# Block-causal attention and a two-layer FFN on one core: pairs of heads in float32 on the two column halves, joined maxima and sums, and six blocks in the end phase

## The chip, the cores and the metric

The kernel runs on one core of a Trainium2 chip. TensorE (PE) multiplies matrices out of SBUF into PSUM (8 banks of 128 partitions x 512 float32), VectorE (DVE), ScalarE (ACT) and GpSimd (POOL) work element by element, and SyncE (SP) issues the DMAs. Each engine takes its instructions in the order in which the program wrote them and waits on semaphores for the others. The metric is the device time of one execution in microseconds (us); lower is better. All inputs and outputs are float32.

## The reference

Attention over 8 batches x 8 heads, 576 positions of 64, with a mask in blocks of 64; then an FFN with silu over the 4608 tokens.

```python
def attn(q, k, v):                            # (8, 8, 576, 64) float32
    scores = np.matmul(q, k.transpose(0, 1, 3, 2)) / 8
    block = np.arange(576) // 64
    scores = np.where(block[:, None] >= block[None, :], scores, -1e9)
    p = np.exp(scores - scores.max(-1, keepdims=True))
    return np.matmul(p / (p.sum(-1, keepdims=True) + 1e-9), v)

def reference(q, k, v, moe_w_in, moe_w_out):  # (512, 2048), (2048, 512)
    x = attn(q, k, v).transpose(0, 2, 1, 3).reshape(4608, 512)
    h = x @ moe_w_in
    return (h / (1 + np.exp(-h))) @ moe_w_out
```

## The kernel before

**Precision.** Almost every product is taken as three products of rounded parts: a float32 operand is split into a high part (a cast to fp32r on ACT) and a low part (the difference, on POOL), and PE adds high x high, high x low and low x high.

**Attention.** The first 128 queries of each head are done early by the classes First and Second. The other 448 queries of a head are a unit; there are 64 units (u0 to u63), two heads that are neighbours being a pair. Keys lie on the partitions, queries along the free axis, five segments of keys (SEG) of 448, 320, 192, 448 and 64 queries. A unit goes through these steps:
- load (L290): q and k from DRAM into qkraw, of which there is one buffer, in two halves; split_hi (L298, ACT), split_lo (L302 and L304, POOL): qh and ql.
- scores (L326, PE): into three PSUM banks S.
- max (L270, DVE): for each segment a reduction with transposition over 32 keys into Mx; max2: quad_fold (L279) joins the four quarters of the partitions in four reductions, four more (L341) write the result to each quarter, and a broadcast (L274) fills MR.
- sub (L351, L356, L358, DVE): T = S - MR; exp (L367, ACT): p; p_hi (L373, ACT) and p_lo (L381, L383, POOL): ph, pl; v_hi (L310) and v_lo (L313): vc, with the low part of v beside the high part in the columns.
- sums (L270 into Dx, DVE), and once per pair sums2 (L279 into Xd, L396, L398): the reciprocal rr.
- pv (L405, PE): nine matmuls into U, high parts in one half of its partitions, low in the other; lower (L410, ACT) and fold (L416, DVE) add the halves; mult (L274, L421, DVE) multiplies by rr.
- x_hi (L450), x_lo (L456): the FFN's operand x, in 16 tiles that are free again once their block is done. For blocks in LATER x goes to DRAM instead.

**FFN.** 18 blocks of 256 tokens. A step is 12 matmuls of the first layer (L652, into h) or of the second (L687, into o); between them stand silu (L659), g_hi (L665) and g_lo (L670). 14 blocks go step by step beside the attention, 448 steps in all. The other four (LATER) wait for the end phase.

**Order.** Up to unit 16 a table (ORDER) says what each engine's queue gets, word by word. From TABLE = 17 a loop writes one unit after the other and puts FFN steps among them: `pace` is what is left to reach an even share, three of them at the end of the unit, and `while len(x_free) < z.fresh(): ffn(1)` does more where no x tile is free. The steps that remain after the loop are written ahead of the end phase.

**End phase.** For the blocks put off, two layers with seven products in place of eight (Strassen's scheme in Winograd's form, on halves of the operands). First layer: an item (L1000) is seven products of six matmuls into PSUM tiles X, Y (both named S) and Z; ACT copies partial sums out (keep, L1005), DVE and POOL add (L849), ACT applies silu (L1013). Second layer: mult_c (L1111). The sums of operands that the scheme needs are made by prep_x, prep_s, prep_t and prep_g (L849 sums and low parts, L858 casts). Everything in this phase is written as `at(t, ...)` with a planned time t and then sorted by it; ITEM = 4.94 is the planned length of an item, and product 1 of an item opens the PSUM tile that the item before last used.

Of the kernel before, what the change touches and what calls it, by code (L numbers as in the profile page):

```python
# [20 lines left out]
P = 128  # L21
# [7 lines left out]
TB = 256  # L29
# [6 lines left out]
TABLE = 17  # L36
LAG = 2
LATER = (14, 15, 16, 17)
# [5 lines left out]
USE = (1, 2, 6, 5, 7, 3, 4)  # L44
# [81 lines left out]
u15.lower u18.load ffn u16.p_hi:0 u15.fold u16.p_hi:1 u16.p_lo:0 u16.v_hi u15.mult ffn u16.v_lo ffn silu u16.p_lo:1 u17.load_v  # L126
g_hi u16.p_hi:2 ffn g_lo u15.x_hi ffn u15.x_lo silu ffn u16.p_lo:2 g_hi g_lo
# [14 lines left out]
def attn_ffn(ctx: ExitStack, tc: tile.TileContext, qk, v, qk0, v0, qk1, v1, w_in, w_out, out):  # L142
# [138 lines left out]
    class Unit:  # L281
# [10 lines left out]
        def load_v(u):  # L292
            u.vraw = sp.tile([P, 512], F32, tag="vraw", name="vraw")[:, : 5 * D]
            nc.sync.dma_start(out=u.vraw, in_=v[u.b, u.h])
# [40 lines left out]

        def max2(u):
            X = sp.tile([32, NQB, 4], F32, tag="Xm", name="Xm")
            quad_fold(X, Mx, ALU.max)
            m = sp.tile([P, NQB], F32, tag="m", name="m")
            for a in range(4):  # L340
                nc.vector.tensor_reduce(out=m[32 * a : 32 * a + 32], in_=X, axis=AX.X, op=ALU.max)  # L341
            u.mb = MR[:, :NQ]
            bcast(u.mb, m, NQB)
# [41 lines left out]
        def sums(u):  # L385
            n = u.h % 2 * NQB
            for j, c, q0, w in SEG:
                ttr(Dx[:, n + q0 // 32 : n + q0 // 32 + w // 32, j], blocks32(u.p[:, c : c + w]), ALU.add)
# [11 lines left out]
        def pv(u):  # L400

            U = u.U = pU.tile([P, 512], F32, tag="U", name="U")[:, :NQ]
            for n, (i, pp, m) in enumerate(PV):
                j, c, q0, w = SEG[i]
                nc.tensor.matmul(U[:m, q0 : q0 + w], u.vc[:, j, :m], (u.ph, u.pl)[pp][:, c : c + w], start=n == 0, stop=n == 8)  # L405

# [286 lines left out]
    def output(blk, d, t):  # L693
        ot = sp.tile([P, DM], F32, tag="ot", name="ot", bufs=2)
        ((o, c),) = outs[blk][t]
        (nc.vector.tensor_copy if late else nc.scalar.copy)(ot, o)
# [38 lines left out]
    late = []  # L735
# [24 lines left out]
    units = [Unit(b, h) for b in range(B) for h in range(H)]  # L760
    for i in range(0, len(units), 2):
# [22 lines left out]
    total = 4 * len(steps)  # L784
    for i in range(TABLE, n + 2):
        u = units[i] if i < n else None
        w = units[i - 1] if i <= n else None
        z = units[i - 2] if i > TABLE else None
        pace = AHEAD + (total - TAIL - AHEAD) * (i + 1 - TABLE) // (n + 2 - TABLE) - count[0]
# [15 lines left out]
        if z and z.h % 2:  # L805
# [4 lines left out]
        if w:  # L810
            w.sums()
            w.pv()
        if u:
            u.v_hi()
            u.v_lo()
            if i + 1 < n:
                units[i + 1].load_v()
            u.sub()
        if w:
            w.lower()  # L820
        if u:
            for part in (u.exp, u.p_hi, u.p_lo):
                for k in range(3):
                    part(k)
        if w and w.h % 2:
            w.sums2()
        late.append(u)
        ffn(3)
        late.pop()
# [7 lines left out]
    for i in range(left):  # L837
        at(FULL * (i - left), ffn, 1)
# [7 lines left out]
    right = {}  # L846

# [9 lines left out]
    def parts(t, h, l, src, eng, lag=0.9):  # L857
# [3 lines left out]
    def ops(t, e, out, a, b, op):  # L861
        at(t, lambda: tt(e, out(), a(), b(), op))

# [23 lines left out]
    def prep_x(t, u):  # L887
# [8 lines left out]

        b11, b12, b21, b22 = q(0, 0), q(0, 1), q(1, 0), q(1, 1)

        def t2():
            if u:  # L900
                z["t"] = right["p"].tile([P, 2, TB], F32, tag="tx", name="tx")
            return z["t"] if u else b22()

        def hl(t, j, src, eng):
            p = pair(u, j)
            if u:
                t = max([t] + [u * span - ITEM + (USE.index(i) + 1) * ITEM / 7 + 0.02 for i in USE if ring[u - 1][i] == ring[u][j]])
            parts(t, p[:, :, 0], p[:, :, 1], src, eng)

        at(t, load, 0)  # L910
        at(t, load, 1)
        hl(t + 4.0, 1, b11, V)
        hl(t + 4.7, 2, b21, G)
        ops(t + 5.6, V, b11, b12, b11, SUB)
        hl(t + 5.4, 3, b22, V)
        ops(t + 6.3, V, b12, b22, b12, SUB)
        ops(t + 7.0, V, t2, b22, b11, SUB)
        two_ = (lambda: z["t"]) if u else b22
        ops(t + 7.7, V, b21, b21, two_, SUB)
        hl(t + 7.7, 6, two_, G)  # L920
        hl(t + 8.4, 5, b11, V)
        hl(t + 9.1, 7, b12, G)
        hl(t + 9.8, 4, b21, V)

    def prep_s(t, d):
# [3 lines left out]
        h21, l21 = [w[:, 0:2, cols(d, 1)] for w in wi]  # L929
        at(t, raw, z, 0)  # L930

        def q(i, j=None):
            return lambda: z[0].rearrange("p q (c m) -> p q c m", c=2)[:, i : i + 1 if j is None else j]

        def whole(f):
            tt((G, V)[f], z[0][:, 2 * f : 2 * f + 2].rearrange("p q (c m) -> p (q c) m", c=2), f32(wi[0][:, :, cols(d, f)]), f32(wi[1][:, :, cols(d, f)]), ADD)

        at(t, whole, 0)
        at(t, whole, 1)
        ops(t + 0.9, V, q(3), q(2), q(3), ADD)  # L940
        ops(t + 1.4, V, q(2), q(0), q(2), SUB)
        ops(t + 1.8, V, q(0), q(3), q(0), SUB)
        ops(t + 2.3, V, q(1), q(1), q(0), SUB)
        parts(t + 1.4, h21, l21, lambda: q(3)()[:, 0], V, 1.6)
        parts(t + 2.8, H, L, q(0, 3), G)

    def prep_t(t, d):
# [3 lines left out]
        B = [w[:, 2 * d : 2 * d + 2, :].rearrange("p f (n m) -> p (f n) m", n=2) for w in wo]  # L951
        at(t, raw, z, 0)

        def q(i, j=None):
            return lambda: z[0][:, i : i + 1 if j is None else j]

        at(t, lambda: tt(G, z[0], f32(B[0]), f32(B[1]), ADD))
        ops(t + 2.6, V, q(0), q(1), q(0), SUB)
        ops(t + 3.0, V, q(1), q(3), q(1), SUB)
        ops(t + 3.5, V, q(3), q(3), q(0), SUB)  # L960
        ops(t + 3.9, V, q(2), q(2), q(3), SUB)
        parts(t + 3.5, H[:, 0:2], L[:, 0:2], q(0, 2), V)
        parts(t + 4.4, H[:, 2:4], L[:, 2:4], q(2, 4), G)
# [11 lines left out]
    def item(t, u, d, k):  # L975
        z = {}
        e = d % HALFD
        stat = {
            1: [w[:, 0:2, cols(d, 0)] for w in wi],
            2: [w[:, 2:4, cols(d, 0)] for w in wi],  # L980
            4: [w[:, 2:4, cols(d, 1)] for w in wi],
            5: [w[:, 0:2, cols(d, 1)] for w in wi],
            6: [w[:, e, 0] for w in sv],
            3: [w[:, e, 1] for w in sv],
            7: [w[:, e, 2] for w in sv],
        }

        def prod(i, o):
            if i == 1:
                z["X"] = bank(k % 2)[:, :TB]  # L990
                z["g"] = [both(k) for k in range(2)]
            elif i == 2:
                z["Y"] = bank(2)[:, :TB]
            elif i == 5:
                z["Z"] = pU.tile([P, 512], F32, tag="U", name="Z")[:, :TB]
            x = pair(u, i)
            n = 0
            for c in range(2):
                for a, b in ((0, 0), (0, 1), (1, 0)):
                    nc.tensor.matmul(z[o], stat[i][a][:, c], x[:, c, b, :], start=i in (1, 2, 5) and n == 0, stop=n == 5, skip_group_check=True)  # L1000
                    n += 1

        def keep(e, name, o):
            z[name] = half("s1" if name == "s5" else name)
            (e.copy if e is A else e.tensor_copy)(z[name], z[o])  # L1005

        def add(e, q, a, b):
            tt(e, z["g"][q[0]][:, q[1]], z[a], z[b], ADD)

        def silu2(h):  # L1010
# [10 lines left out]
        p = ITEM / 7  # L1021
        for n, (i, o) in enumerate(((1, "X"), (2, "Y"), (6, "X"), (5, "Z"), (7, "X"), (3, "Z"), (4, "X"))):
            at(t + n * p, prod, i, o)
        at(t + p + 0.01, keep, A, "s1", "X")
        at(t + 2 * p + 0.01, add, V, (0, 0), "Y", "s1")
        at(t + 2.6 * p, silu2, 0)
        at(t + 3 * p + 0.01, keep, A, "s2", "X")
        at(t + 4 * p + 0.01, keep, V, "s5", "Z")
        at(t + 5 * p + 0.01, keep, A, "s3", "X")
        at(t + 5.6 * p, add, G, (1, 1), "s5", "s3")  # L1030
        at(t + 6 * p + 0.01, add, V, (1, 0), "Z", "s2")
        at(t + 6 * p + 0.45, silu2, 1)
        at(t + 7 * p + 0.1, save, 1)
        at(t + 7 * p + 0.15, silu21)
        at(t + 7 * p + 0.5, save, 0)

    at(-0.005, start_b)
    for u in range(nuse):
        if u == 0 or order[u] != order[u - 1]:
            prep_x(u * span - 14.0, u)  # L1040
        for e in range(HALFD):
            d = e + HALFD * (u >= NDBL)
            t = u * span + e * ITEM
            if u in (0, NDBL):
                prep_s(t - 6.5 - (u > 0) * 1.5, d)
            item(t, u, d, u * HALFD + e)
    for d in range(HALFD):
        prep_t(end_b - span - 13.0 + 6.0 * d, d)
        prep_t(end_b - span + 11.0 + 5.5 * d, HALFD + d)

    flat = lambda z: z.rearrange("p a b c -> p (a b c)")
    et = lambda z: z.rearrange("p (j e t) -> p j e t", e=2, t=P)
# [15 lines left out]
    def prep_g(t, blk, q, c, tag):  # L1068
# [135 lines left out]
```

## Time and profile before

| what | us |
|---|---|
| median of 2 runs | 1151.69 (1150.3 to 1153.09) |
| the profiled execution, its own time | 1154.32 |
| its span | 1152.6 |
| PE busy | 1057.3 |
| DVE busy | 948.2 |
| POOL busy | 829.2 |
| ACT busy | 793.9 |

The span is the time from the first instruction to the last in the profiled execution, and the execution's own time is 1.7 us longer. The mean granted clock of PE is 0.967 of full speed. Rows of groups read: line, engine, operation, output <- input by the program's names, shape, count, then busy time, mean ns of one, and the idle time before them with what ended it. L12 is line 12 of the kernel.

### The profile page before, as it was taken

Reading aid. Unit: us, or ns where it says so; the run is one execution under the profiler, and the core shown is the slowest. Engines: PE = TensorE matmul, PEld = TensorE weight load, DVE = VectorE, ACT = ScalarE, POOL = GpSimd, SP = SyncE. Lnnn points to the kernel's source line nnn. Section 1 sums busy time; section 2 is a strip of 40 time slices with the busy share of each in tenths; the row PEclk is TensorE's granted clock in tenths of the full one; section 3 lists DMA queues with packets and bytes.
Section 4 is the critical chain, followed back from the end, with each engine's and each line's share of the span. In section 5 each row is a group of like instructions: output and inputs, shape, how many; then the busy total and the mean of one; then the engine's idle time right before and its main releaser. Section 6 shows DMA issues by size and latency. Waiting matters only on the chain.

```text
span 1152.6 us, 21493 instructions
## 1 busy us (share of the span) xinstructions
PE 1057.3 (92%) x7348; PEld 966.5 (84%) x7348; DVE 948.2 (82%) x2513; ACT 793.9 (69%) x1294; POOL 829.2 (72%) x751
## 2 busy tenths in 40 slices
PE   9999999999989997999999779999999787677987
PEld 8888999999978886889989669889889687577887
DVE  7986799999699996999985789999992757879665
ACT  5776688889788877888884768888873454443332
POOL 5766699889969886798976678878773646655344
PEclk9999999999999998999999889999999899788999
DMA  7873333232232321313221222332312033132431
GB/s 272 274 251 107 80 82 82 59 82 59 63 91 49 90 57 41 90 49 92 67 73 45 55 71 66 84 88 58 99 46 64 22 124 107 48 121 66 119 92 56
DMA packets 61389, 102.06 MB, mean 89 GB/s; under 512 B 7264, under 2 KB 34400, under 8 KB 61280
## 3 DMA queue, kind: packets, MB, share of 16 engines
q1 hardware_dynamic: 61280, 100.69, 30.9%
q8 instruction: 58, 0.95, 0.3%
q14 instruction: 51, 0.42, 0.1%
HBM read 80.74 MB, written 19.92 MB: 87 GB/s over the span
## 4 chain that ended last, share of the span: by engine, by line
PE 45%; DVE 28%; issue 8%; ACT 7%; POOL 7%; DMA 4%; SPq 2%; POOLq 0%; DVEq 0%; ACTq 0%
PE h L652 15%; PE o L687 15%; PE U L405 5%; PE S L326 4%; DVE Mx L270 3%; DVE Dx L270 3%; DVE raw L849 3%; PE S L1000 2%; DVE rx L849 2%; DVE m L341 1%; DVE Xm L279 1%; DVE xu L416 1%; ACT p L367 1%; POOL pl L381 1%; DVE MR L274 1%
## 5 line engine op out<-in xcount | busy, mean ns | idle before, releaser
L652 PE MATMUL h<-x,wi 128*128 128x256 f32 x2688 | 349.5, 284 | 0.0
L652 PEld LDWEIGHTS h<-x,wi 128*128 128x128 f32 x2688 | 339.8, 191 | 8.5 <-issue 0.5
L687 PE MATMUL o<-wo,g 128*128 128x512 f32 x1296 | 328.9, 399 | 0.0
L381 POOL TENSOR_TENSOR pl<-p,ph 128x448 fp32r<-128x448 f32 (+1 forms) x192 | 225.7, 1202 | 86.6 <-ACT ph L373 86.5
L687 PEld LDWEIGHTS o<-wo,g 128*128 128x128 f32 x1296 | 238.5, 190 | 48.6 <-issue 0.7
L670 POOL TENSOR_TENSOR g<-g,g 128x512 fp32r<-128x512 f32 x112 | 145.4, 1298 | 57.9 <-ACT g L665 42.7
L270 DVE TRANSPOSE_TENSOR_REDUCE Mx<-S 64x4 f32<-64x128 f32 (+4 forms) x384 | 132.9, 401 | 57.2 <-PE S L326 57.0
L270 DVE TRANSPOSE_TENSOR_REDUCE Dx<-p 128x14 f32<-128x448 f32 (+3 forms) x320 | 122.5, 445 | 0.1
L367 ACT ACTIVATE p<-T 128x512 f32<-128x512 f32 (+1 forms) x192 | 106.9, 605 | 19.7 <-POOL ph L383 14.0
L405 PE MATMUL U<-ph,vc 128*128 128x448 f32 (+3 forms) x320 | 78.8, 312 | 34.4 <-DVE xu L421 22.3
L302 POOL TENSOR_TENSOR qh<-qkraw,qh 64x576 fp32r<-64x576 f32 x64 | 91.7, 1433 | 18.0 <-ACT qh L298 9.1
L373 ACT CAST ph<-p 128x512 fp32r<-128x512 f32 (+1 forms) x192 | 104.0, 596 | 0.7 <-PE U L405 0.5
L659 ACT ACTIVATE g<-h 128x512 f32<-128x512 f32 x112 | 67.0, 598 | 47.4 <-POOL g L670 31.6
L367 ACT ACT_TABLE_LOAD x60 | 77.0, 1283 | 28.1 <-DVE T L356 26.8
L405 PEld LDWEIGHTS U<-ph,vc 128*128 128x128 f32 x320 | 59.1, 196 | 44.0 <-POOL ph L383 27.9
L326 PE MATMUL S<-qh 128*128 128x448 f32 (+3 forms) x320 | 91.1, 297 | 1.0 <-DVE T L356 0.7
L665 ACT CAST g<-g 128x512 fp32r<-128x512 f32 x112 | 69.4, 620 | 22.2 <-PE o L687 20.2
L326 PE MATMUL S<-ql,qh 128*128 128x448 f32 (+3 forms) x320 | 83.8, 306 | 0.0
L659 ACT ACT_TABLE_LOAD x64 | 82.1, 1283 | 1.1
L298 ACT CAST qh<-qkraw 128x1024 fp32r<-128x1024 f32 x64 | 66.8, 1044 | 16.8 <-DMA qkraw<-in_qk_dram 13.4
L304 POOL TENSOR_TENSOR ql<-qkraw,qh 128x448 fp32r<-128x448 f32 x64 | 74.1, 1158 | 5.0
L358 DVE TENSOR_TENSOR T<-S,MR 128x256 f32<-128x256 f32 (+2 forms) x192 | 72.9, 405 | 0.0
(206 smaller groups left out, 1959.5 us busy)
## 6 DMA issues: line engine op xcount, KB each, us to landing
qkraw<-in_qk_dram SPq DMA_DIRECT2D x128, 256.0 KB, 3.9
vraw<-in_v_dram SPq DMA_DIRECT2D x64, 160.0 KB, 3.0
gd<-g SPq DMA_DIRECT2D x32, 256.0 KB, 2.1
wst<-in_moe_w_out_dram SPq DMA_DIRECT2D x15, 512.0 KB, 5.0
rx<-gd SPq DMA_DIRECT2D x44, 128.0 KB, 2.7
wst<-in_moe_w_in_dram SPq DMA_DIRECT2D x10, 512.0 KB, 5.2
out_dram<-ot SPq DMA_DIRECT2D x17, 256.0 KB, 2.9
v<-in_v_dram SPq DMA_DIRECT2D x12, 256.0 KB, 5.9
```

What stands on the lines that cost most here:

```text
L270: nc.vector.tensor_reduce(out=out, in_=in_, axis=AX.X, op=op, apply_transpose=True)
L302: nc.gpsimd.tensor_tensor(out=u.qh[64:, NQ:], in0=u.raw[64:, NQ:], in1=u.qh[64:, NQ:], op=ALU.subtract)
L304: nc.gpsimd.tensor_tensor(out=u.ql, in0=u.raw[:, :NQ], in1=u.qh[:, :NQ], op=ALU.subtract)
L326: nc.tensor.matmul(u.ps(c, w, m), u.kk[:, j * P : j * P + m], qq[:, q0 : q0 + w], start=i == 0, stop=i == 1)
L367: nc.scalar.activation(u.p[:, c:e], T[:, c:e], AF.Exp, scale=SCALE)
L373: nc.scalar.copy(u.ph[:, c:e], u.p[:, c:e])
L381: nc.gpsimd.tensor_tensor(out=u.pl[:, c:e], in0=u.p[:, c:e], in1=u.ph[:, c:e], op=ALU.subtract)
L405: nc.tensor.matmul(U[:m, q0 : q0 + w], u.vc[:, j, :m], (u.ph, u.pl)[pp][:, c : c + w], start=n == 0, stop=n == 8)
L652: nc.tensor.matmul(h[:, f, :], wi[wt][:, c, w], x[:, xt, :], start=n == 0, stop=n == 3 * CT - 1)
L659: nc.scalar.activation(g, hs.pop((blk, d)), AF.Silu)
L670: nc.gpsimd.tensor_tensor(out=g2[:, 1], in0=g, in1=g2[:, 0], op=ALU.subtract)
L687: nc.tensor.matmul(o, g2[:, gt, f, tk], wo[wt][:, 2 * d + f, c], start=d == 0 and n == 0, stop=d == NSTEP - 1 and n == 5,)
```

## The change

From unit 16 on (PAIRED) neither p nor v is split. p stays in float32, in three buffers in turn (those that p, ph and pl had), and pv2 multiplies both heads of a pair at once: each head's v (64 columns) takes one half of PE's columns. U then holds both heads, and neither lower nor fold is needed. Maxima: one reduction over Mx (max_x), three copies on POOL that bring the other three quarters of the partitions beside the first (gather), one reduction (max_m), three copies back. Sums: the same with sums_x, gather and sums_m, where POOL also adds. split_lo of the next unit comes after these instead of before the FFN steps. mult2 multiplies out of PSUM. `late` becomes `by_vector`, and `late` now counts the steps at the unit's end.

Six blocks are put off instead of four: 384 FFN steps remain in the loop, and the end phase has 24 items in each layer instead of 16. Its products come in the order 1, 6, 5, 2, 7, 3, 4, with product 1 of an item three slots earlier, among the last products of the item before. The sums of prep_x, prep_s, prep_t and prep_g are written into PSUM (quad, with hold and wait to plan who has which bank), low parts from there are made by DVE, and most additions move to DVE.

```diff
-LATER = (14, 15, 16, 17)
+PAIRED = 16
+LATER = (12, 13, 14, 15, 16, 17)
-USE = (1, 2, 6, 5, 7, 3, 4)
+USE = (1, 6, 5, 2, 7, 3, 4)
...
+        def gather(u, z):
+            for a in range(1, 4):
+                nc.gpsimd.tensor_copy(out=z[:32, a], in_=z[32 * a : 32 * a + 32, 0])
+
+        def max_x(u):
+            u.mj = MR[:, 448:504].rearrange("p (a b) -> p a b", a=4)
+            nc.vector.tensor_reduce(out=u.mj[:, 0], in_=Mx, axis=AX.X, op=ALU.max)
+
+        def max_m(u):
+            u.m = sp.tile([P, NQB], F32, tag="m", name="m")
+            nc.vector.tensor_reduce(out=u.m[:32], in_=u.mj[:32].rearrange("p a b -> p b a"), axis=AX.X, op=ALU.max)
+            for a in range(1, 4):
+                nc.gpsimd.tensor_copy(out=u.m[32 * a : 32 * a + 32], in_=u.m[:32])
...
+        def sums_x(u):
+            u.dj = ident[:, : 8 * NQB].rearrange("p (a b) -> p a b", a=4)
+            nc.vector.tensor_reduce(out=u.dj[:, 0], in_=Dx, axis=AX.X, op=ALU.add)
+
+        def sums_m(u):
+            z, rs = u.dj, sp.tile([P, NQB], F32, tag="rs", name="rs")
+            t = MR[:32, 960:1016].rearrange("p (a b) -> p a b", a=2)
+            u.rs = rs
+            nc.gpsimd.tensor_tensor(out=t, in0=z[:32, 0:2], in1=z[:32, 2:4], op=ALU.add)
+            nc.gpsimd.tensor_scalar(out=t[:, 0], in0=t[:, 0], scalar1=1e-9, scalar2=None, op0=ALU.add)
+            for a in range(4):
+                n = slice(NQB * (a // 2), NQB * (a // 2) + NQB)
+                nc.gpsimd.tensor_tensor(out=rs[32 * a : 32 * a + 32], in0=t[:, 0, n], in1=t[:, 1, n], op=ALU.add)
...
-                u.p = sp.tile([P, COLS], F32, tag="p", name="p")
+                u.p = sp.tile([P, COLS], F32, tag=("p", "ph", "pl")[max(0, u.i - PAIRED) % 3], name="p")
...
+        def pv2(u):
+
+            U = u.U = pU.tile([P, 512], F32, tag="U", name="U")[:, :NQ]
+            for n, (j, c, q0, w) in enumerate(SEG[i] for i in (0, 3, 1, 2, 4)):
+                for e, z in enumerate((u.mate, u)):
+                    nc.tensor.matmul(U[64 * e : 64 * e + 64, q0 : q0 + w], z.vv[:, j], z.p[:, c : c + w], start=n == 0, stop=n == 4)
+
+        def mult2(u):
+
+            bc = MR[:, 512 : 512 + NQ]
+            bcast(bc, u.rr, NQB)
+            u.xu = sp.tile([P, 512], F32, tag="xu", name="xu")[:, :NQ]
+            nc.vector.tensor_tensor(out=u.xu, in0=u.U, in1=bc, op=ALU.mult)
...
-        pace = AHEAD + (total - TAIL - AHEAD) * (i + 1 - TABLE) // (n + 2 - TABLE) - count[0]
+        pace = max(0, AHEAD + (total - TAIL - AHEAD) * (i + 1 - TABLE) // (n + 2 - TABLE) - count[0])
+        late = min(pace, 2 if i % 2 == 0 else 3)
         if u:
             u.scores()
             u.max()
-        if z:
-            z.fold()
-            if z.h % 2:
-                z.mult()
-        if u:
-            u.max2()
-        if i + 1 < n:
-            units[i + 1].split_hi()
-            units[i + 1].split_lo()
+            u.max_x()
+            u.gather(u.mj)
+        if nxt:
+            nxt.split_hi()
             if i + 2 < n:
                 units[i + 2].load()
-        ffn(pace - 3)
...
+        ffn(pace - late)
+        if w:
+            w.sums(2)
+        if u:
+            u.max_m()
+        if w:
+            w.sums(-3)
+        if done:
+            done.pv2()
+            done.sums_x()
+            done.gather(done.dj)
+            done.sums_m()
+        if nxt:
+            nxt.split_lo()
+        if u:
+            u.max_b()
+            u.sub()
+        if z:
+            z.sums_r()
+            z.mult2()
...
+    def quad(t, z, q, kind, where, outs):
...
+        t = wait(where, t)
+        hold(where, t + 3.15)
+        at(t, start)
+        if kind == "S":
+            ops(t + 0.5, V, x(0), x(3), q(3), ADD)
+            ops(t + 0.9, V, x(1), q(0), x(3), SUB)
+            ops(t + 1.3, V, x(2), x(0), q(0), SUB)
+            ops(t + 1.7, V, x(3), q(1), x(2), SUB)
...
+        for i, o in ((1, "X"), (6, "X"), (5, "Z"), (2, "Y"), (7, "X"), (3, "Z"), (4, "X")):
+            at(t + USED[i] * p7 - ITEM * (i == 1), prod, k, i, o)
```

Where instructions stand now, at three places. POOL's queue through one unit of the steady loop, before (pl and ph: the low parts of p; g: that of the FFN's g; qh and ql: those of the next unit's k and q; vc: that of v):

```order
L302 TENSOR_TENSOR qh<-qkraw,qh 64x576
L304 TENSOR_TENSOR ql<-qkraw,qh 128x448
L313 TENSOR_TENSOR vc<-vraw,vc 128x5x64
L381 TENSOR_TENSOR pl<-p,ph 128x448
L381 TENSOR_TENSOR pl<-p,ph 128x512
L381 TENSOR_TENSOR pl<-p,ph 128x448
L383 TENSOR_TENSOR ph<-p,ph 64x64
L670 TENSOR_TENSOR g_7766<-g,g_7766 128x512
L302 TENSOR_TENSOR qh<-qkraw,qh 64x576
```

and after, in an even unit (MR holds the maxima of the four quarters, m the joined ones, ident the sums, rs their total):

```order
L352 COPY MR<-MR 32x14 x3
L362 COPY m<-m 32x14 x3
L352 COPY ident<-ident 32x28 x3
L376 TENSOR_TENSOR MR<-ident 32x56
L377 TENSOR_SCALAR MR<-MR 32x28
L380 TENSOR_TENSOR rs<-MR 32x14 x4
L316 TENSOR_TENSOR qh<-qkraw,qh 64x576
L318 TENSOR_TENSOR ql<-qkraw,qh 128x448
```

The low parts of p and v are gone; qh and ql, which the next unit's scores read, now stand behind fifteen small operations on maxima and sums.

PE's queue from the end of unit 28's scores, before (S: scores, U: p times v, h: FFN):

```order
L326 MATMUL S_5894<-ql,qh 64x64
L405 MATMUL U<-ph,vc 128x448
L405 MATMUL U<-ph,vc 128x320
L405 MATMUL U<-ph,vc 128x192
L405 MATMUL U<-pl,vc 64x192
L405 MATMUL U<-pl,vc 64x320
L405 MATMUL U<-pl,vc 64x448
L405 MATMUL U<-ph,vc 128x64
L405 MATMUL U<-pl,vc 64x448
L405 MATMUL U<-ph,vc 128x448
L652 MATMUL h<-x,wi_78 128x256 x2
```

and after, from the end of unit 30's scores to the start of unit 31's:

```order
L340 MATMUL S_5806<-ql,qh 128x192
L340 MATMUL S_5807<-qh 64x64
L340 MATMUL S_5807<-ql,qh 64x64
L462 MATMUL U<-p,v 64x448 x4
L462 MATMUL U<-p,v 64x320 x2
L462 MATMUL U<-p,v 64x192 x2
L462 MATMUL U<-p,v 64x64 x2
L340 MATMUL S_5880<-qh 128x448
```

Before, FFN steps follow the product p·v; after, no step stands between the scores of unit 28 and those of unit 32 but the products of a pair, as 25 steps were written into unit 27.

PE's queue at the end of an item of the first layer, before (Z and S: the PSUM tiles; the second S number is the next item's):

```order
L1000 MATMUL Z<-x,sv_11387 128x256 x2
L1000 MATMUL Z<-x,sv_11388 128x256
L1000 MATMUL S_11589<-x,wi_78 128x256 x2
L1000 MATMUL S_11589<-x,wi_79 128x256
L1000 MATMUL S_11589<-x,wi_78 128x256 x2
L1000 MATMUL S_11589<-x,wi_79 128x256
L1000 MATMUL S_11660<-x,wi_78 128x256 x2
L1000 MATMUL S_11660<-x,wi_79 128x256
L1000 MATMUL S_11660<-x,wi_78 128x256 x2
```

and after:

```order
L1127 MATMUL S_10013<-x,wi_78 128x256 x2
L1127 MATMUL S_10013<-x,wi_79 128x256
L1127 MATMUL S_10013<-x,wi_78 128x256 x2
L1127 MATMUL S_10013<-x,wi_79 128x256
L1127 MATMUL Z<-x,sv_9748 128x256 x2
L1127 MATMUL Z<-x,sv_9749 128x256
L1127 MATMUL Z<-x,sv_9748 128x256 x2
L1127 MATMUL Z<-x,sv_9749 128x256
L1127 MATMUL S_9955<-xown,wi_78 128x256 x2
L1127 MATMUL S_9955<-xown,wi_79 128x256
L1127 MATMUL S_9955<-xown,wi_78 128x256 x2
```

Product 1 of the next item (S_10013) now stands ahead of products 3 (Z) and 4 (S_9955) of the item before; it had stood behind both.

More of the change, by code (lines that the diff above doesn't have):

```diff
@@ L760, in attn_ffn @@
     units = [Unit(b, h) for b in range(B) for h in range(H)]
+    for i, u in enumerate(units):
+        u.i = i
     for i in range(0, len(units), 2):
@@ L809, in attn_ffn @@
             z.x_lo()
[L810 to L829, printed above, removed]
+        by_vector.append(u)
+        ffn(late)
+        by_vector.pop()
     events = []
@@ L913, in prep_x @@
[L913 to L925, printed above, removed]
+        at(t + 4.0, start)
+        hl(t + 4.2, 1, b11, G)
@@ L926, in prep_s @@
+        for _ in range(2):
+            hold("rx", max(ends) + 0.05)
+    def prep_s(t, d, where):
         z = {}
@@ L973, in both @@
         return right["p"].tile([P, 2, TB], F32, tag=f"g{k}", name=f"g{k}", bufs=2 - k)
[L975 to L988, printed above, removed]
+    items = [{} for _ in range(nuse * HALFD)]
@@ L998, in prod @@
[L998 to L1008, printed above, removed]
```

300 lines of the change are left out of this document (189 added, 111 removed).

## The prediction

> **What bounds the kernel now.** I read the page first (busy shares, chain), then the busy time of every engine stretch by stretch, then a steady unit on the timeline, then the waits of the last phase. The page's first part and its chain:
>
> ```profile
> PE 1057.3 (92%) x7348; PEld 966.5 (84%) x7348; DVE 948.2 (82%) x2513; ACT 793.9 (69%) x1294; POOL 829.2 (72%) x751
> PE 45%; DVE 28%; issue 8%; ACT 7%; POOL 7%; DMA 4%; SPq 2%; POOLq 0%; DVEq 0%; ACTq 0%
> ```
>
> PE is nearest to full, but the chain runs through DVE for 28%: the average mixes stages. The view by stretches (start:end, length, then PE, PEld, DVE, ACT, POOL busy, then the granted clock), cut at the first score matmuls of units 17 and 63, the end phase's first product, and its second layer:
>
> ```profile
> 310.90:853.60 542.70, 506.85 (x3203) 459.13 (x3202) 478.30 (x1499) 433.52 (x668) 432.29 (x420) 0.98 0.27 69
> 853.60:906.00 52.40, 52.40 (x319) 46.56 (x318) 28.19 (x63) 24.76 (x42) 25.32 (x22) 1.00 0.14 43
> 906.00:1040.10 134.10, 99.02 (x674) 94.15 (x673) 99.82 (x151) 62.48 (x144) 75.99 (x52) 0.88 0.27 91
> 1040.10:1152.60 112.50, 91.12 (x673) 87.45 (x672) 77.84 (x118) 33.03 (x58) 51.42 (x28) 0.92 0.29 85
> ```
>
> Up to 853.6 PE is the bound (507 of 543 us). In the last two stretches nothing is full: PE works 99 of 134 us at clock 0.88. There 16 items of seven products take 8.4 us each, then 16 of the second layer 7.0, the last stores among them. Two starts of product 1 (each row joins product 1 and its neighbour) show what an item without a stall costs, 5.2 us, and the waits of 905 to 1152 (us in total, times, longest) what stalls the others:
>
> ```profile
> 948.06 1.60 PE L1000 MATMUL S<-x,wi 128*128 128x256 f32 x12
> 953.26 1.60 PE L1000 MATMUL S<-x,wi 128*128 128x256 f32 x12
> PEld S L1000 <- ACT s L1005: 22.5, 14, 5.7
> PE Z L1000 <- DVE s L1005: 15.7, 8, 3.0
> POOL x L849 <- ACT x L858: 31.2, 11, 3.8
> ```
>
> **PE work of the loop.** A steady unit on PE's timeline (start, us, line, shape, count):
>
> ```profile
> 712.14 1.56 PE L687 MATMUL o<-wo,g 128*128 128x512 f32 x6
> 713.54 0.60 PE L405 MATMUL U<-ph,vc 128*128 128x448 f32 x3
> ...
> 714.87 1.56 PE L687 MATMUL o<-wo,g 128*128 128x512 f32 x6
> 716.26 3.04 PE L652 MATMUL h<-x,wi 128*128 128x256 f32 x24
> 719.14 0.36 PE L326 MATMUL S<-qh 128*128 128x448 f32 x1
> ...
> 720.54 0.71 PE L687 MATMUL o<-wo,g 128*128 128x512 f32 x2
> ```
>
> By starts, an FFN step is 1.39 to 1.44 us (6 matmuls of L687 in 713.54 - 712.14 or 716.26 - 714.87; 24 of L652, two steps, in 719.14 - 716.26): I take 1.42. The product p·v costs 714.87 - 713.54 = 1.33, I take 1.40 for it and for the scores (720.54 - 719.14).
>
> The new product issues ten float32 matmuls once per pair, head by head into the two column halves. A float32 matmul is two records. The nearest rows:
>
> ```profile
> 116.91 1.15 PE L628 MATMUL S<-p,v 128*64 128x64 f32 x32
> 17.42 1.03 PE L468 MATMUL idle<-zero 128*64 128x64 f32 x14
> ```
>
> Where halves alternate, a record of 64 columns takes 1.15/32 = 36 ns (about 30 between starts), in one half alone 1.03/14 = 74 (about 62). So two halves do run together. A pair has 2 x 1472 columns of four quarter-rate passes; scaled from 30 ns per 64 columns of a record this is 2 x 1472/64 x 2 x 30 ns = 2.76 us, from the longer matmuls' rate 2.45: I take 2.6. Bounds: 2.45 and 5.7 (halves one after the other). Before it was 2 x 1.40: no gain for PE.
>
> Two more blocks put off: 64 FFN steps fewer in the loop, 64 x 1.42 = 91 us, and 8 more items in each layer of the end phase, which at 5.2 us each take 83. So the change is nearly neutral in PE work; the gain must come from stalls.
>
> **The other engines, per unit.** From the second stretch, per unit (47 of them): POOL 9.2, ACT 9.2, DVE 10.2 of 11.5 us. The groups that go or come in another order, by shape, and DVE's timeline of a unit:
>
> ```profile
> L381 POOL TENSOR_TENSOR pl<-p,ph 128x448 fp32r<-128x448 f32 x128 | 148.0, 1157 | 86.6 <-ACT ph L373 86.5
> L383 POOL TENSOR_TENSOR ph<-p,ph 64x64 fp32r<-64x64 f32 x64 | 20.3, 318 | 5.0
> L302 POOL TENSOR_TENSOR qh<-qkraw,qh 64x576 fp32r<-64x576 f32 x64 | 91.7, 1433 | 18.0 <-ACT qh L298 9.1 <-issue 3.1 <-POOL g L670 1.2
> L304 POOL TENSOR_TENSOR ql<-qkraw,qh 128x448 fp32r<-128x448 f32 x64 | 74.1, 1158 | 5.0
> L298 ACT CAST qh<-qkraw 128x1024 fp32r<-128x1024 f32 x64 | 66.8, 1044 | 16.8 <-DMA qkraw<-in_qk_dram 13.4 <-PE S L326 2.4 <-POOL pl L381 0.9
> 717.35 1.18 DVE L279 TENSOR_REDUCE Xd<-Dx 32x28 f32<-32x140 f32 x4
> 718.56 0.90 DVE L396 TENSOR_REDUCE rs<-Xd 32x14 f32<-32x70 f32 x4
> 719.74 0.65 DVE L270 TRANSPOSE_TENSOR_REDUCE Mx<-S 128x14 f32<-128x448 f32 x1
> 720.65 1.50 DVE L270 TRANSPOSE_TENSOR_REDUCE Mx<-S 128x8 f32<-128x256 f32 x5 [0.26 <-PE S L326]
> 722.19 0.63 DVE L416 TENSOR_TENSOR xu<-U,t 64x448 f32<-64x448 f32 x1
> 724.08 0.90 DVE L279 TENSOR_REDUCE Xm<-Mx 32x14 f32<-32x70 f32 x4
> 725.01 0.85 DVE L341 TENSOR_REDUCE m<-Xm 32x14 f32<-32x56 f32 x4
> ```
>
> DVE loses per pair 2 x (0.90 + 0.85 + 0.63) + 1.18 + 0.90 = 6.8 us. It gains five reductions of some 0.22 us (a quarter of the Xm row): 1.1. From 20.4 it comes to about 15 us per pair. ACT loses three casts of p and those of v and U, POOL the low parts of p (two of 1.16 us, a longer one, and 0.32) and of v. None of these was on the path except through DVE and through `U <- pl`.
>
> New on POOL are small operations: 6 per unit for the maxima (copies from one quarter of the partitions to another) and 9 per pair for the sums. The trace has none so small. From 1157 ns at 448 and 318 at 64 elements the slope is 2.19 ns and the rest 0.18 to 0.21 us; with the hand-over to the next I take 0.28, bounds 0.15 (half of 318) and 0.5 (it waits for each predecessor). What matters is where they stand: ahead of the low part of the next unit's q and k (L302, L304), which the next scores need.
>
> So a unit has a new loop: scores, maxima, POOL's copies, the low part, next scores. From 719.14 to 722.15, where the last Mx ends, are 3.0 us; the two joined reductions with three hand-overs between DVE and POOL 0.8; 15 small operations 4.2 (six in the odd units: 1.7); the low part 1.43 + 1.16 and its hand-overs 2.8. Even unit 10.9 us, odd 8.3. In the odd units there is also the load, since q and k have one buffer, freed by the low part:
>
> ```profile
> qkraw<-in_qk_dram SPq DMA_DIRECT2D x128, 256.0 KB, 3.9
> ```
>
> 3.9 for a half, 0.6 until the second is issued, 1.04 for the cast, 2.8: 8.4 us. I take 10.9 and 8.4, 19.3 per pair.
>
> Against this stands PE's own time with the FFN steps that the new order puts into each unit: in the order of PE's instructions units 17 to 62 get 198 steps, but 58 of them in three bursts (units 23, 27, 35: 11, 25, 22), because room for x tiles is made there; after each the pace is zero, and twelve units (17, 24, 25, 28 to 32, 36 to 39) have two steps or none. With 1.40 + 1.42 per step + 2.6 in even units, and each unit as long as the larger of that and its loop, the 46 units sum to 507 us (PE alone: 405). The twelve have PE waiting 4 to 9 us in each, and that costs clock:
>
> ```profile
> 593.46 0.82 PE L405 MATMUL U<-ph,vc 128*128 128x448 f32 x3 [2.23 <-DVE xu L421]
> ...
> 595.74 2.25 PE L687 MATMUL o<-wo,g 128*128 128x512 f32 x6
> ```
>
> After a gap of 2.23 us six L687 take 2.25 us instead of 1.56. In the twelve units the scores then take up to 2.8 us instead of 1.4; where the loop is the bound, this lies on the path. Some of the gaps fall short, so I take 0.8 us for each, 10 us in all.
> The Trainium skill ("TensorE: Matmul & The Clock Gate", Part 1) says that the array falls to half its clock after at least one idle window of about 3.4 us, and that the windows run freely; the trace shows the fall after 2.23 us. By that rule every one of the twelve would be at half clock, 12 x 1.4 = 17 us in place of 10, and the time 7 us longer.
>
> Loop from unit 17 to 63: 517 us, against 542.7. Bounds: 481 + 5 (small operations of 0.15: 8.9 in even units, while the load still holds the odd ones at 8.4) and 546 + 10 (halves one after the other).
>
> **The tail of the loop.** Unit 63 keeps 30 steps: 1.4 + 2.6 + 30 x 1.42 = 46.6, before 52.4.
>
> **The end phase.** 24 items per layer. Product 1 is issued three slots early, so that a PSUM half is read during two slots (1.5 us) and not one (0.74) before PE writes it again: the waits of S for ACT and of Z for DVE lose their cause, since the copy takes 0.37 (row below). The sums that prepare operands are made in PSUM:
>
> ```profile
> L849 DVE TENSOR_TENSOR raw<-raw 128x256 f32<-128x256 f32 x84 | 55.2, 657 | 3.9 <-POOL raw L849 1.9
> L849 DVE TENSOR_TENSOR g<-S,s 128x256 f32<-128x256 f32 x18 | 7.6, 423 | 21.4 <-ACT s L1005 8.9 <-PE S L1000 6.8 <-ACT s L1122 3.0
> L1005 ACT COPY s<-S 128x256 f32<-128x256 f32 x48 | 17.7, 368 | 14.8 <-PE S L1000 14.5
> ```
>
> 657 becomes 423 for each. POOL's long low parts (`x L849 <- ACT x`, 31 us of waits) go to DVE in pieces. Adding up at such prices what the new order gives each engine between two items, DVE has some 4.6 us and ACT 4.75 per item of the first layer against PE's 5.2, which is tight: where operands of a second or third pair of blocks are prepared, ACT is full, and that gives the next stall. I take 5.6 per item of both layers, the last stores among them: 48 x 5.6 = 269. Bounds: 48 x 5.2 = 250, and 24 x (8.38 + 7.03) = 370 at the present rates.
>
> **The sum.** 310.9 + 517 + 46.6 + 269 = 1143.5 us of span. The profiled execution took 1154.32 for its span of 1152.6, so 1.7 more: 1145.2. It lies 2.6 over the median of 1151.69, so 1142.6; I say 1142. (From the span to the median, then, it is -0.9.)
>
> **Rivals.**
> (a) Faster. Small operations take 0.15 us, and the end phase runs at 5.3 per item: 310.9 + 486 + 46.6 + 254 - 0.9 = 1097; with the first alone 1112, with the second alone 1128. For it: the waits of the end phase name just what is removed. Against it: the low part and the load remain.
> (b) Slower: the end phase keeps its rate per item, because the stall only changes its place (ACT full). Then 370 in place of 269: 1244. It decides from 6.3 us per item, where both layers pass 301. For it: 4.75 of 5.2. Against it: items at 5.2 already occur.
> (c) The change does not do what it says, as the halves don't run together: 5.7 in place of 2.6 per pair, the loop 546 + 10, the tail + 3: 1185. Against it: the row of L628.
> (d) Small POOL operations take 0.5 us each: loops of 14.2 and 9.6, 605 us: 1230. For it: no row is so small. Against it: 318 ns for 64 elements.
>
> **Chances.** My forecast 0.57 (own range 1115 to 1172), (a) 0.20, (b) 0.08, (c) 0.08, (d) 0.07. A measurement here tells 2% from no change: below 1128.7 is faster, above 1174.7 slower. Faster: 0.20 and 0.17 of the forecast's lower part, 0.37. Slower: (b), (d) and half of (c), 0.19. Same: 0.44. For the range: (b) and (d) may act in part, so about half of them lies beyond 1192, and a twentieth below 1092.
>
> **What the profile after would show.** Right: L462 takes about 2.6 us per pair; the score matmuls of even paired units start 10.5 to 11.5 us before the next, with POOL's low part (L316, L318) ending just ahead of them; twelve units without FFN, PE's clock at 0.5 there; first-layer items of 5.4 to 6.0 us with no wait of PE for ACT's copies over 1 us. Wrong: PE without gaps in those units (a); `S <- ACT s` waits as long as before (b); L462 near 5.5 us (c); POOL rows L352, L362 of 0.5 us (d).

## The result and the profile after

The changed kernel takes 1211.11 us (median of 2 runs, 1210.3 to 1211.91) against 1151.69: 1.052 times the time before, interval 1.045 to 1.058. It is slower; the forecast was 1142 with a range up to 1192. The profiled execution has a span of 1208.3 us. The page's first part, after:

```profile
PE 1078.0 (89%) x7492; PEld 948.2 (78%) x7492; DVE 819.4 (68%) x2135; ACT 692.5 (57%) x1153; POOL 651.0 (54%) x987
```

DVE, ACT and POOL are 101 to 178 us less busy than before, as meant, and still the kernel is longer. The view by stretches of the same profile, cut at the same places (start:end, length, then PE, PEld, DVE, ACT and POOL busy, then PE's clock):

```profile
310.60:892.50 581.90, 473.04 (x2710) 384.04 (x2708) 361.62 (x1016) 285.61 (x381) 291.65 (x648) 0.88 0.27 64
892.50:945.60 53.10, 49.71 (x282) 42.63 (x282) 19.81 (x47) 21.64 (x36) 19.47 (x29) 0.95 0.14 44
945.60:1078.00 132.40, 125.62 (x1009) 122.11 (x1010) 85.97 (x194) 90.04 (x228) 51.24 (x37) 1.00 0.41 138
1078.00:1208.30 130.30, 122.87 (x1010) 121.25 (x1008) 87.59 (x195) 57.31 (x129) 48.59 (x47) 1.00 0.40 114
```

The end phase did what it was changed for: 24 items a layer in 132 and 130 us, 5.5 us an item, PE busy for 94 to 95% at full clock; where PE's weight loads waited 22.5 us in all for ACT's copies before, from 945 to 1208 us they now wait 4.6, and 1.3 at the longest

```profile
PEld S L1127 <- ACT s L1137: 4.6, 7, 1.3
```

The loss is all in the first row: units 17 to 63 take 582 us instead of 543, though they hold 60 FFN steps fewer (198 for 258), and no engine but PE is busy for more than 63% of it. Its waits (us in total, times, longest), from 310 to 893:

```profile
DVE Mx L271 <- PE S L340: 162.0, 71, 28.2
ACT qh L312 <- DMA qkraw<-in_qk_dram: 146.1, 34, 7.0
POOL MR L352 <- DVE MR L356: 107.3, 38, 4.4
POOL g L734 <- ACT g L729: 99.0, 37, 4.4
...
PE S L340 <- POOL qh L316: 88.4, 30, 5.5
ACT p L417 <- DVE T L406: 61.5, 31, 2.9
DVE MR L275 <- POOL m L362: 50.1, 15, 5.2
```

DVE waits for PE's scores, PE for the low part of q and k (POOL), POOL for ACT, ACT for the load, DVE for POOL. One unit shows how these hang together. Unit 52 has four FFN steps and lasts 14.9 us (starts of the scores). PE's timeline (start, us, line, shape, count, and in brackets the idle time before and its releaser), then those of SP's queue, ACT and POOL:

```profile
757.09 0.37 PE L340 MATMUL S<-qh 128*128 128x448 f32 x1
...
758.62 3.05 PE L751 MATMUL o<-wo,g 128*128 128x512 f32 x12
761.60 2.70 PE L462 MATMUL U<-p,v 128*64 128x448 f32 x20
764.23 3.13 PE L716 MATMUL h<-x,wi 128*128 128x256 f32 x24
771.95 0.74 PE L340 MATMUL S<-qh 128*128 128x448 f32 x1 [4.58 <-POOL qh L316]
773.16 0.74 PE L340 MATMUL S<-ql,qh 128*128 128x448 f32 x1 [0.47 <-POOL ql L318]
```

```profile
757.29 1.12 SPq L291 DMA_DIRECT2D qkraw<-in_qk_dram  x2
...
773.13 1.11 SPq L291 DMA_DIRECT2D qkraw<-in_qk_dram  x2
```

```profile
762.10 1.04 ACT L312 CAST qh<-qkraw 128x1024 fp32r<-128x1024 f32 x1 [2.29 <-DMA qkraw<-in_qk_dram]
763.16 1.28 ACT L723 ACT_TABLE_LOAD   x1
764.46 0.60 ACT L723 ACTIVATE g<-h 128x512 f32<-128x512 f32 x1
765.09 0.62 ACT L729 CAST g<-g 128x512 fp32r<-128x512 f32 x1
```

```profile
756.11 1.16 POOL L318 TENSOR_TENSOR ql<-qkraw,qh 128x448 fp32r<-128x448 f32 x1
759.89 1.29 POOL L734 TENSOR_TENSOR g<-g,g 128x512 fp32r<-128x512 f32 x1 [2.63 <-ACT g L729]
761.25 0.64 POOL L352 COPY MR<-MR 32x14 f32<-32x14 f32 x3
765.85 1.29 POOL L734 TENSOR_TENSOR g<-g,g 128x512 fp32r<-128x512 f32 x1 [3.97 <-ACT g L729]
767.21 0.65 POOL L362 COPY m<-m 32x14 f32<-32x14 f32 x3
767.92 0.68 POOL L352 COPY ident<-ident 32x28 f32<-32x28 f32 x3
768.67 0.29 POOL L376 TENSOR_TENSOR MR<-ident 32x56 f32<-32x56 f32 x1
769.05 0.27 POOL L377 TENSOR_SCALAR MR<-MR 32x28 f32<-32x28 f32 x1
769.40 1.01 POOL L380 TENSOR_TENSOR rs<-MR 32x14 f32<-32x14 f32 x4
770.50 1.40 POOL L316 TENSOR_TENSOR qh<-qkraw,qh 64x576 fp32r<-64x576 f32 x1
771.97 1.13 POOL L318 TENSOR_TENSOR ql<-qkraw,qh 128x448 fp32r<-128x448 f32 x1
```

Read it as a ring. The low part ends at 757.27 and frees qkraw; the load is issued at 757.29 and lands by 762.10; ACT casts. Behind the cast, in ACT's queue, stand the silu and the cast of the FFN's g (its h was complete before the scores began): until 765.71. Only then can POOL make the low part of g (L734, called g_lo, as the cast is called g_hi), and it stands in POOL's queue ahead of the copies of the maxima, of the sums, and of the low part of q and k, which ends at 773.10. The next load is issued at 773.13: 15.8 us from load to load, in which PE has 9.7 us of work (1.4 + 4 x 1.42 + 2.6).

### The profile page after: what moved, and what is told of

Its sections match the earlier page's. It is cut to its first block, busy times and chain, and to the rows that moved or that the text cites. A ratio compares the mean times of both kernels' runs of the same rounds, so it can differ in the third digit from the quotient of the medians.

```text
span 1208.3 us, 21677 instructions
## 1 busy us (share of the span) xinstructions
PE 1078.0 (89%) x7492; PEld 948.2 (78%) x7492; DVE 819.4 (68%) x2135; ACT 692.5 (57%) x1153; POOL 651.0 (54%) x987
## 5 line engine op out<-in xcount | busy, mean ns | idle before, releaser
L716 PE MATMUL h<-x,wi 128*128 128x256 f32 x2304 | 306.1, 288 | 0.0
L716 PEld LDWEIGHTS h<-x,wi 128*128 128x128 f32 x2304 | 296.1, 195 | 7.8 <-issue 0.5
L751 PE MATMUL o<-wo,g 128*128 128x512 f32 x1104 | 290.5, 409 | 0.0
L751 PEld LDWEIGHTS o<-wo,g 128*128 128x128 f32 x1104 | 208.4, 196 | 43.4 <-issue 0.5
L734 POOL TENSOR_TENSOR g<-g,g 128x512 fp32r<-128x512 f32 x96 | 123.9, 1290 | 158.1 <-ACT g L729 143.8
L340 PEld LDWEIGHTS S<-qh 128*128 128x128 f32 (+1 forms) x320 | 68.1, 213 | 99.9 <-POOL qh L316 97.3
L340 PEld LDWEIGHTS S<-ql,qh 128*128 128x128 f32 (+1 forms) x320 | 68.3, 213 | 36.7 <-POOL ql L318 33.0
L352 POOL COPY MR<-MR 32x14 f32<-32x14 f32 x141 | 26.2, 186 | 116.1 <-DVE MR L356 111.7
L275 DVE STREAM_TRANSPOSE MR<-m 128x448 f32<-128x448 f32 x64 | 40.2, 628 | 55.3 <-POOL m L362 54.6
L462 PE MATMUL U<-p,v 128*64 128x448 f32 (+3 forms) x480 | 70.3, 441 | 1.4 <-DVE xu L469 1.4
```

Source lines behind the costliest of these rows:

```text
L340: nc.tensor.matmul(u.ps(c, w, m), u.kk[:, j * P : j * P + m], qq[:, q0 : q0 + w], start=i == 0, stop=i == 1)
L462: nc.tensor.matmul(U[64 * e : 64 * e + 64, q0 : q0 + w], z.vv[:, j], z.p[:, c : c + w], start=n == 0, stop=n == 4)
L716: nc.tensor.matmul(h[:, f, :], wi[wt][:, c, w], x[:, xt, :], start=n == 0, stop=n == 3 * CT - 1)
L734: nc.gpsimd.tensor_tensor(out=g2[:, 1], in0=g, in1=g2[:, 0], op=ALU.subtract)
L751: nc.tensor.matmul(o, g2[:, gt, f, tk], wo[wt][:, 2 * d + f, c], start=d == 0 and n == 0, stop=d == NSTEP - 1 and n == 5,)
```

## The experiments

The theory to test is this ring (load, cast, silu and g_hi on ACT, g_lo, small operations, low part on POOL, load). Rivals: the small operations on POOL are dear; the late copies hold DVE up; the bursts and the units without FFN steps are the loss; six blocks are too many. All ratios below are against the kernel before, timed beside each run: there it took 1154.5 to 1156.5 us, where it took 1151.69 beside the changed kernel, so that differences in us from the changed kernel are uncertain by 3 to 5 us.

**e1: the maxima ahead of the FFN steps.**

```diff
-        ffn(pace - late)
         if w:
             w.sums(2)
         if u:
             u.max_m()
+        ffn(pace - late)
```

> Edit of the changed kernel: the joined maxima (max_m and its three copies on POOL) are written ahead of the FFN steps of the unit, so that the g_lo of those steps no longer stands ahead of the copies on POOL. The low part of q and k stays behind the g_lo. Ring theory (the time of a unit is a ring: load of q and k, their cast on ACT, silu and g_hi behind it on ACT, g_lo, the small operations, the low part of q and k, which frees the buffer for the next load): the copies leave the ring, but the rest stays, 0.7 us less in each of some 25 units: about 1190 to 1205 us. Rival (what costs is DVE's wait for the late copies of m, 50 us in all in the changed kernel's list of waits): about 1160 us.

Measured: 1202.25 us (ratio 1.041, 1.039 to 1.044). As the ring says: the copies are early now, and little is gained, 9 us. DVE's wait for them, 50.1 us in the list above, is gone from this run's list, so that it was not the cost.

**e2: the low part of q and k ahead of them too.**

```diff
+        if w:
+            w.sums(2)
+        if u:
+            u.max_m()
         if nxt:
             nxt.split_hi()
+            nxt.split_lo()
...
         ffn(pace - late)
-        if w:
-            w.sums(2)
-        if u:
-            u.max_m()
...
-        if nxt:
-            nxt.split_lo()
```

> Edit of the changed kernel: as e1_copies_first, and the low part of q and k also stands ahead of the FFN steps and of the sums, right behind its cast, where it stood before the change. Ring theory: the ring is cut, only load, cast and low part are left in it (8.4 us), a unit takes the larger of that and PE's work, units 17 to 63 take about 485 us instead of 582: about 1115 us. Rival (the small operations on POOL and the units without FFN steps are the loss, and the place of g_lo matters little): no more than 4 us less per pair, about 1165 us or above.

Measured: 1111.49 us (0.963, 0.961 to 0.964), faster than the kernel before. Units 17 to 63 take 486.2 us. One place in the order of POOL's queue (the low part now ahead of the g_lo and of the sums' small operations) is worth 91 us from e1 to e2. The loop's row and the waits that are left:

```profile
310.30:796.50 486.20, 436.24 (x2709) 361.78 (x2708) 359.78 (x1016) 283.57 (x379) 292.29 (x640) 0.94 0.33 77
ACT qh L312 <- DMA qkraw<-in_qk_dram: 84.0, 33, 4.8
PE S L340 <- POOL qh L316: 30.0, 7, 6.1
```

The three engines beside PE are as busy as in the changed kernel, to 2 us; PE's wait for the low part fell from 88 to 30 us.

**e3: no bursts, no units without steps.**

```diff
-LATER = (12, 13, 14, 15, 16, 17)
+LATER = (6, 9, 12, 15, 16, 17)
```

> Edit of the changed kernel: other blocks are put off, 6, 9, 12, 15, 16 and 17, so that every unit from 18 on has 4 or 5 FFN steps and none has a burst or is without. Ring theory: every unit then goes at the rate of the units 40 to 62 of the changed kernel, 258.5 / 22 = 11.75 us, units 17 to 63 take about 535 us instead of 582: about 1165 us. Rival (the bursts and the starved units are the loss, and a steady unit takes half of the 19.3 us that were forecast for a pair): about 440 us, so 1070 us.

Measured: 1180.21 us (1.022, 1.020 to 1.024). Of what was lost it gives back 31 us, less than the ring theory's 46 and far from the rival's 140: with its FFN steps spread evenly the loop still takes 548.5 us, and the units that had no g_lo in their ring now have one too:

```profile
310.70:859.20 548.50, 460.79 (x2710) 375.25 (x2708) 362.72 (x1016) 307.19 (x401) 295.83 (x653) 0.93 0.29 67
```

**e4: four blocks put off.**

```diff
-LATER = (12, 13, 14, 15, 16, 17)
+LATER = (14, 15, 16, 17)
```

> Edit of the changed kernel: four blocks put off as before the change (14 to 17); the loop in pairs and the new end phase stay. Ring theory: with 5 or 6 steps in a unit PE's work (8.5 to 12.5 us) is a smaller part behind the ring, units take 12 to 13 us; the end phase loses 16 of 48 items of 5.5 us (88 us), the loop gains 64 steps: about 1190 to 1215 us. Rival (the six blocks are what costs, by starving units of FFN steps): the loop no slower than before the change, 543 us, and the end phase 175 us: about 1075 to 1090 us.

Measured: 1177.73 us (1.020, 1.018 to 1.023), 12 us below what the ring theory gave. But it parts the change in two, with as many blocks put off as before:

```profile
311.70:938.00 626.30, 545.15 (x3250) 450.28 (x3248) 364.04 (x1016) 336.98 (x448) 318.38 (x675) 0.94 0.25 60
993.20:1087.20 94.00, 85.65 (x672) 81.91 (x673) 66.30 (x154) 62.94 (x163) 43.50 (x31) 1.00 0.38 127
1087.20:1176.10 88.90, 82.10 (x674) 80.89 (x672) 59.86 (x133) 38.78 (x87) 32.78 (x31) 1.00 0.37 108
```

Units 17 to 63 take 626.3 us against 542.7 before, 84 more; the end phase takes 182.9 against 246.6, 64 less.

**e6: e2 and e3 together.**

> Edits of the changed kernel: e2_low_part_first and e3_spread together. Ring theory: with the ring cut, a unit takes what it took in the steady units of e2_low_part_first (10.0 and 8.6 us, or 12.0 and 7.2, so 18.9 a pair), now for all of them, without units that have no FFN steps: units 17 to 63 about 435 to 440 us instead of 486, in all about 1062 us. Rival (the spread gains the same 31 us as in e3_spread, which is what the bursts cost in any case): about 1080 us.

Measured: 1067.72 us (0.923, 0.921 to 0.926). With the ring cut, spreading the steps is worth 44 us (31 with the ring), nearer to the theory's 50 than to the rival's 31:

```profile
310.20:751.20 441.00, 423.97 (x2709) 352.79 (x2709) 359.48 (x1016) 304.53 (x399) 294.79 (x645) 0.98 0.36 84
```

**e7: the new end phase alone**, with the old loop, where p and v are split and nothing is paired; four blocks are put off.

> The kernel before with the new end phase alone: four blocks put off, no pairing. If the end phase gains by itself what e4_four_blocks shows for 16 items a layer (134.1 + 112.5 us against 94.0 + 88.9), then 64 us less: about 1090 us. Rival (its waits were hidden by the loop's earlier end, or it needs the paired loop): within 20 us of 1152.

Measured: 1091.71 us (0.945, 0.942 to 0.947), so the end phase gains alone what e4 showed:

```profile
909.20:1002.10 92.90, 85.22 (x672) 81.81 (x673) 66.29 (x154) 63.07 (x163) 43.45 (x31) 1.00 0.39 128
1002.10:1091.00 88.90, 82.12 (x674) 80.91 (x672) 59.80 (x133) 38.63 (x87) 32.76 (x31) 1.00 0.37 108
```

**e8: q and k loaded twice** in the changed kernel.

```diff
-            for r in (0, 64):
+            for r in (0, 64) * (1 + (u.i > TABLE + 1)):
```

> Edit of the changed kernel: q and k of units 19 to 63 are loaded twice, with four DMAs in a row instead of two, and nothing else. Ring theory: the load is a link of the ring, two more issues of 0.55 us, about 1.1 us or more in each of some 36 to 45 units: 1250 us or more. Rival (the load is hidden behind the FFN steps, and ACT would wait for something else): 1211 us as before.

Measured: 1341.35 us (1.161, 1.158 to 1.164). The load is a link: one more costs 130 us, 2.9 for each of 45 units. Each is dearer than I had put it, as SP's queue shows: four DMAs now take 4.94 to 5.01 us to issue, where two take 1.1. In the first row below the second pair starts at 873.04 us, 3.5 after the first; it seems to wait until the first has landed, which no run tests. And ACT's wait for the load grew from 146 to 325 us:

```profile
869.50 5.01 SPq L291 DMA_DIRECT2D qkraw<-in_qk_dram  x4
886.84 4.94 SPq L291 DMA_DIRECT2D qkraw<-in_qk_dram  x4
ACT qh L312 <- DMA qkraw<-in_qk_dram: 324.5, 39, 11.6
```

**e9: the sums' small operations behind the low part.**

```diff
-            done.gather(done.dj)
-            done.sums_m()
         if nxt:
             nxt.split_lo()
+        if done:
+            done.gather(done.dj)
+            done.sums_m()
```

> Edit of the changed kernel: the gather of the sums and sums_m, nine small operations on POOL per pair, stand behind the low part of q and k instead of ahead of it; the g_lo stay where they were. Ring theory: the 2.9 us that they take are a link of the ring in the even units, which are some 20 with FFN steps, so 45 to 60 us less: 1150 to 1165 us. Rival (only the g_lo and the copies of the maxima are late): less than 15 us gained, about 1200 us.

Measured: 1156.53 us (1.001, 0.999 to 1.002), 55 us less than the changed kernel: the nine operations are a link of the ring too. (In unit 52's rows they take 2.5 us, 767.92 to 770.41.) That the gain met its range is in part luck: 36 of the 55 us fall in the 31 units with 4 or 5 FFN steps, and 18 in the twelve with two or none (115.1 to 96.8 us), which the expectation did not count. In unit 30, one of these, POOL's queue holds no g_lo, and the cast ends at 491.17 us, 3.6 before the low part starts (494.79): what holds such a unit is the loop that the prediction had, through maxima and small operations.

**e10: six blocks with the old loop.** As e7, without the pairs' part of the change.

```diff
-LATER = (14, 15, 16, 17)
+LATER = (6, 9, 12, 15, 16, 17)
```

> As e7_end_phase_alone (the loop before the change, without pairs, and the new end phase), with six blocks put off, 6, 9, 12, 15, 16 and 17, so that 4 or 5 FFN steps stand in each unit. What it asks is what the pairs are needed for. If DVE bounds a unit of the old loop that has few FFN steps (in the kernel before the units 44 and 45 take 9.3 and 14.1 us), the loop doesn't get shorter, 46 x 11.7 = 538 us, and eight more items a layer make it 1165 us. If the old loop follows PE's work (6.9 to 8.4 us and 1.4 more a unit), it is about 450 us and the whole 1080 us, no worse than e6_low_part_spread.

Measured: 1158.53 us (1.003, 1.001 to 1.004). Taking 64 steps out of the old loop shortens it by only 19 us (544.8 to 525.5). DVE is the fullest engine, busy for 90% of it, and of PE's own waits the longest in total is for DVE:

```profile
310.70:836.20 525.50, 450.86 (x2664) 398.58 (x2663) 474.03 (x1491) 414.53 (x629) 407.91 (x395) 0.94 0.28 70
PE U L455 <- DVE xu L485: 51.4, 21, 4.2
```

DVE has 474 us of work there against 359 in the paired loop of e6. Pairs and e2's order together buy 91 us with six blocks (e10 to e6). That this is room on DVE is read from these rows and not shown alone: the pairs also relieve ACT and POOL (415 and 408 us to 305 and 295).

**e11: e2's order with four blocks put off.**

```diff
-LATER = (12, 13, 14, 15, 16, 17)
+LATER = (10, 15, 16, 17)
```

> Edit of the changed kernel: the order of e2_low_part_first with four blocks put off, 10, 15, 16 and 17, so that units 18 to 62 have 5 or 6 FFN steps. Ring theory: with 5 or 6 steps PE's work of a unit (8.5 to 9.9 us in odd units, 11.1 to 12.5 in even ones) covers the 8.4 us that are left of the ring; units 17 to 63 take PE's sum, 262 x 1.42 + 46 x 1.4 + 23 x 2.6 = 496 us and a little, the end phase 183: about 1050 us. Rival (six blocks are better once the ring is cut, since they take 91 us of steps out of the loop for 83 in the end phase): 1070 us or more.

Measured: 1055.3 us (0.914, 0.913 to 0.916), the best of all, 36 us less than with the old loop and as many blocks (e7). PE is the bound in the loop at full clock, and over the whole span:

```profile
310.90:815.70 504.80, 500.52 (x3250) 427.88 (x3249) 361.91 (x1016) 335.85 (x453) 319.45 (x680) 1.00 0.32 74
```

```profile
PE 1029.1 (98%) x7396; PEld 915.7 (87%) x7396; DVE 773.2 (73%) x2035; ACT 697.3 (66%) x1119; POOL 655.2 (62%) x997
```

**e12: the cast of q and k behind silu on ACT**, POOL's order untouched.

```diff
-        if nxt:
-            nxt.split_hi()
-            if i + 2 < n:
-                units[i + 2].load()
         ffn(pace - late)
+        if nxt:
+            nxt.split_hi()
+            if i + 2 < n:
+                units[i + 2].load()
```

> Edit of the changed kernel: the cast of q and k on ACT (and the load of the unit after) is written behind the unit's FFN steps instead of ahead of them, so that silu and g_hi no longer stand on ACT behind a cast that waits for the load; POOL's order stays. Ring theory: this takes the link on ACT out of the ring (load to g_lo); in unit 52 g_hi could start at 761.6 us, when its second step has ended, instead of 765.1, so that some 2.5 us fall away in each of about 25 units: 1135 to 1165 us. Rival (the g_lo are late because their FFN steps on PE are, and ACT's order doesn't matter): 1205 us or more.

Measured: 1176.92 us (1.018, 1.015 to 1.020): 34 us less than the changed kernel, not the 46 to 76 I expected, nor nothing. Unit 52 takes 12.5 us, 2.3 less, close to the 2.5 worked out; but only 15 of the units, not 25, got shorter by 0.8 us or more (the mean of these is 2.3). The link on ACT is real; how many units it holds was mis-sized, and why the others gained nothing was not tried.

## Why the prediction was wrong

- **The new loop of a unit: the step that failed.** The prediction let a unit be as long as the largest of PE's work, of a loop through scores, maxima, small operations and the low part (10.9 us in even units), and of load, cast and low part (8.4 us, in odd ones). It put nothing between the cast and the low part: the load had no part in even units, and the FFN's chain on ACT and POOL was left beside both loops. All of it stands in one ring: the low part of g waits on ACT behind a cast that waits for the load, and the low part of q and k, which frees the buffer for the next load, waits on POOL behind that. In unit 52 the ring takes 15.8 us: load 4.8, cast 1.0, silu and g_hi 2.6, g_lo 1.3, small operations 3.2, low part 2.6, and 0.3 between them. The units say so one class at a time. The twelve with two FFN steps or none sum to 115.1 us, where the working (without clock) gave 115.8. The three bursts took 92.6 for 86.6. The other 31, with 4 or 5 steps, took 374.3 for 304.8: the even ones 13.7 us for 11.0, the odd ones 10.1 for 8.5. That is 69 of the 75 us by which the 46 units exceed 507. e2 moves the low part out of the ring, and the same 31 units take 302.5 us.
- **Rivals.** None of the four named this. (a) failed on the loop, which got longer and not shorter; (b) on the end phase, which didn't keep its rate per item. (c) is refuted by the row of L462: 764.23 - 761.60 = 2.63 us a pair, taken as 2.6. (d) too: three copies take 0.64 to 0.68 us, 0.22 each, where I took 0.28 and (d) 0.5. They cost as a link of the ring (e9: 55 us), not by their price.
- **The end phase** was right: 132.4 + 130.3 = 262.7 us for 269, 5.5 an item for 5.6, and it gives its gain alone (e7). The reason given for 5.6 was not: of an item of the first layer ACT has at most 90.04 / 24 = 3.8 us and DVE 3.6, where 4.75 and 4.6 were counted, so ACT is not full.
- **The other engines' relief** was right: DVE 361.62 / 23 = 15.7 us a pair, taken as 15. Small slips in the working change little: the loop holds 46 units, not 47 (15.1 a pair), the terms of its two loops add to 10.8 and 8.3, and the lower bound of 2.45 for p·v comes out of no row (L687's 1.40 for 6 x 512 columns gives 2.7).
- **The units without FFN steps** have the half clock that was expected. Unit 30's scores, after a gap of 5.12 us, take twice the 0.37 us of unit 52's:

```profile
484.41 0.74 PE L340 MATMUL S<-qh 128*128 128x448 f32 x1 [5.12 <-POOL qh L316]
465.80:505.00 39.20, 18.69 (x83) 12.40 (x81) 28.39 (x81) 11.76 (x17) 19.66 (x52) 0.66 0.24 53
```

  Over the units 28 to 31 (second row) the mean clock is 0.66, though, where 0.5 was named. And the sum of 115.1 has no room for the 10 us that I added for it. That it agrees with 115.8 is in part luck: the even ones right behind a burst (24, 28, 36) take 9.7 us and the others (30, 32, 38) 11.8, for 10.9 each.
- **Two blocks more** were called nearly neutral for PE, which holds only while PE is the bound: with the ring, 64 fewer steps gave 46.5 us (e4 to the changed kernel: loop 626.3 to 581.9, tail 55.2 to 53.1), where 91 were counted, and the end phase took 79.8 us more. With the ring cut, six blocks still take 12 us more than four (e6 and e11).
- **The tail** took 53.1 us for 46.6, 6.5 more, and the end phase 6.3 less. That the two cancel is luck; it leaves the whole miss of the span (1208.3 for 1143.5) in the loop (581.9 for 517).
- **The tests named beforehand**: the low part ending just ahead of the next scores was seen, so was L462 at 2.6 us, and in part the half clock; the longest wait for ACT's copies was 1.3 us (row of L1127), where no more than 1 was named; the 10.5 to 11.5 us per even unit was not seen (13.7 in those with 4 or 5 steps). No named test looked at ACT's queue, where the answer was.

## What to carry to other kernels

When an instruction moves down an in-order queue, follow every instruction now ahead of it back to what releases it, across the other engines, until the chain ends or comes back to the start; if it comes back, the sum around the ring, and not the work of any engine, is the time of an iteration. A buffer with one copy closes such rings easily: put the instruction that frees it ahead of work that waits for something else. And part a change that has two halves: here, with four blocks put off (e4), one half gained 64 us and the other lost 84, and the order of a few lines, with four blocks put off in place of six, made it a kernel 8.6% faster than before.
